# The first batch's attention values loaded once, in pairs of blocks, in a kernel of attention and two feed-forward layers

## The chip, the cores and the metric

The kernel runs on one core of one Trainium2 chip. The metric is the device time of one execution in microseconds: the median was 748.56 us over three runs (747.93 to 750.5). TensorE (PE in the rows) multiplies matrices, VectorE (DVE), ScalarE (ACT) and GpSimd (POOL) do elementwise work, and SyncE (SP) issues most of the DMAs. Each engine takes its instructions in a fixed order, and waits where one of them needs something that another engine or a DMA has not finished.

## The reference

Attention over 4 batches, 8 heads, 576 positions, head size 64, with a causal window of 64 keys; then a gated layer 512 to 2048 to 512, and a second one 512 to 1024 to 512 with a softmax gate and a layer norm. The weights are float64.

```python
rel = pos[:, None] - pos[None, :]
mask = (rel >= 0) & (rel < window)                 # window = 64
scores = np.where(mask, q @ k^T / sqrt(D), -1e9)
attn = softmax(scores);  x = (attn @ v), heads side by side     # 2304 x 512
h = x @ w_in                                       # 512 -> 2048
g = np.where(h >= 1, h, np.where(h <= -1, 0, (h + 1) ** 2 / 4))
x = g @ w_out                                      # 2048 -> 512
h = x @ w_in2;  solu = h * softmax(h)              # 512 -> 1024
out = (layernorm(solu) * g_ln) @ w_out2            # 1024 -> 512
```

## The kernel before

**Tokens.** The 2304 tokens are cut into 12 tiles `t` of 192, three to a batch, and each tile into three blocks `i` of 64 queries. The 8 heads are taken as 4 pairs, so attention has 48 steps `g` (four pairs for each tile); "pair 7" below is the step g=7, the last pair of tile 1. Two tiles make one block `j` of 384 tokens for the first layer.

**Attention of one g.** `st_qkt` transposes q and k (on TensorE while g < 12), `st_s` multiplies a block of 64 queries (of both heads) with the 128 keys that its window can reach: 64 of the block before and its own 64. So one matmul of 128 columns for each `i` (L303), except at a batch's first block, which has only 64 keys. VectorE adds `mask` and takes the row's extreme value (L311), ScalarE exponentiates (L317), VectorE takes the reciprocal of the sum (L327, L328), and GpSimd (g < 12) multiplies by it (`st_norm`, L336). `st_t` transposes the result, and `st_v` multiplies it with the value tile of this block, `vw[t, i]`: 128 keys by 512, the same 64 + 64 keys as in the scores (L370). `load_v(t)` loads a tile's three value tiles. Neighbouring blocks overlap: each of the nine blocks of a batch loads its own 128 keys, although half of them are in the tile before. The rows of 64 floats are 256 bytes each in DRAM. The tag `vw` has six buffers.

**Weights.** The first layer's weights come as 32 units of 512 KB (units are counted from 0; an even unit is a part of `w_in`, the odd one behind it the part of `w_out` for the same `f`). A unit is loaded by SP into one of five buffers `wst` (L113, L115), then turned from float64 into two float32 parts: ScalarE's `split_a` (L121), VectorE's shift and or (L125, L126), ScalarE's copy of the high part (L134), and GpSimd's subtraction for the low part (L135). The subtraction is the last reader: behind it the buffer can take the unit five further on.

**The first layer.** For each `j` and each `f` of 16, `moe_h` makes 12 matmuls into a PSUM buffer `ps_h` (two buffers), the gate runs on VectorE, ScalarE and VectorE (L399, L400, L405), and `moe_y` makes 12 more matmuls into four accumulators. "h(2)" below is `moe_h` for j=0, f=2: the first that takes all 384 tokens, and the first that needs a PSUM buffer back from the earlier gates, so it waits for the max of L405. For j=0 and f = 0, 1 the tokens are taken in two halves. Attention for later tiles and the conversion of the units are laid between these steps (`slot`, `w_conv`, `w_load`).

**Order.** The program is written in one sequence, and a list scheduler then orders each engine's instructions by its own estimate of when each can start. So an edit in one place moves instructions in others, on all engines. On SP the loads go out in one queue: a load that must wait for its buffer holds all behind it.

Of the kernel before, what the change touches and what calls it, by code (L numbers as in the profile page):

```python
# [8 lines left out]
F32 = mybir.dt.float32  # L9
# [11 lines left out]
def kernel(  # L21
# [12 lines left out]
    nc = tc.nc  # L34
    B, H, S, D = q.shape
# [6 lines left out]
    QB = TT // 64  # L42
    NTILES = NT // TT
    TPB = S // TT
# [3 lines left out]
    NF = DFF // 128  # L48
# [10 lines left out]
    mask = const.tile([128, 128], F32, name="mask")  # L59
# [8 lines left out]
    for x in range(2):  # L68
        m = mask[64 * x:64 * x + 64, :]
        nc.gpsimd.affine_select(  # L70
            out=m, in_=m, pattern=[[-1, 128]], compare_op=ALU.is_ge,
# [3 lines left out]
            out=m, in_=m, pattern=[[1, 128]], compare_op=ALU.is_gt,  # L75
# [5 lines left out]
    w_p = ctx.enter_context(tc.tile_pool(name="w", bufs=1))  # L81
    at_p = at_ctx.enter_context(tc.tile_pool(name="at", bufs=2, side="right"))
# [8 lines left out]
    def at_bank(name):  # L91
        if spare:
            spare.append(spare.pop(0))
            if spare[-1] is not None:
                return ps_acc.tile([128, 512], F32, tag=spare[-1], name=name)
        return ps_at.tile([128, 512], F32, tag="a", name=name)
# [52 lines left out]
    wih, wil, woh, wol = {}, {}, {}, {}  # L149
# [62 lines left out]
    qn, kn, qk, vw, qT, kT, xh, xl = {}, {}, {}, {}, {}, {}, {}, {}  # L212
# [5 lines left out]
    def load_qk(g):  # L218
# [29 lines left out]
                    nc.sync.dma_start(out=a[p0:p0 + 32, m0:m0 + n // 32, :], in_=s_[e])  # L248
        qk[g] = a

    def load_v(t):
        b, tl = divmod(t, TPB)
        for i in range(QB):
            w = at_p.tile([128, H, D], F32, tag="vw", bufs=6, name="vw")
            s0 = tl * TT + i * 64 - 64
            if s0 < 0:
                nc.sync.dma_start(out=w[0:64], in_=v[b, :, 0:64, :].rearrange("h p d -> p h d"))
            else:
                nc.sync.dma_start(out=w, in_=v[b, :, s0:s0 + 128, :].rearrange("h p d -> p h d"))
            vw[t, i] = w  # L260
# [2 lines left out]
    q_diag = [at_p.tile([128, QB, 2, 64], F32, bufs=1, name=f"q_diag{z}") for z in range(2)]  # L263
    for z in q_diag:
        nc.vector.memset(z, 0.0)

    def st_qkt(g):
        t, hp = divmod(g, NP)
        qt = qT[g] = q_diag[g % 2]
        kt = kT[g] = at_p.tile([128, TT + 64], F32, tag="kT", name="kT")  # L270
        if g >= NPE:
            a = qk.pop(g)
            for x in range(2):
                s_ = slice(64 * x, 64 * x + 64)
                nc.vector.transpose(qt[s_, :, x, :], a[s_, 0:6, :].rearrange("p m c -> p (m c)"))
            c0 = 0 if t % TPB else 64
            nc.vector.transpose(kt[:, c0:], a[:, 6:14 - c0 // 32, :].rearrange("p m c -> p (m c)"))
            return
        ps = at_bank("ps_t")
        c = 0  # L280
        for src in (qn, kn):
            for r in range(2):
                a = src[t, r]
                n = a.shape[0]
                nc.tensor.transpose(ps[:, c:c + n], a[:, hp * 128:hp * 128 + 128], ident[0:n, 0:n])
                c += n
        psq = ps[:, 0:TT].rearrange("c (i q) -> c i q", i=QB)
        nc.vector.tensor_copy(qt[0:64, :, 0, :], psq[0:64])
        nc.scalar.copy(qt[64:128, :, 1, :], psq[64:128])
        nc.scalar.copy(kt[:, TT + 64 - (c - TT):], ps[:, TT:c])  # L290

    def first(t, i):
        return t % TPB == 0 and i == 0

    def st_s(g):
        t, hp = divmod(g, NP)
        ps = at_bank("ps_s")
        tmp = p = at_p.tile([128, QB, 128], F32, tag="p", bufs=3, name="p")
        mx = at_p.tile([128, QB], F32, tag="mx", name="mx")
        sm = at_p.tile([128, QB], F32, tag="sm", name="sm")  # L300
        for i in range(QB):
            c0 = 64 if first(t, i) else 0
            nc.tensor.matmul(  # L303
                ps[:, i * 128 + c0:i * 128 + 128],
                qT[g][:, i, :, :].rearrange("p x q -> p (x q)"),
                kT[g][:, i * 64 + c0:i * 64 + 128],
                start=True, stop=True,
            )
        for i in range(QB):
            c0 = 64 if first(t, i) else 0  # L310
            nc.vector.tensor_tensor_reduce(  # L311
                out=tmp[:, i, c0:], in0=ps[:, i * 128 + c0:i * 128 + 128], in1=mask[:, c0:],
                scale=-0.125, scalar=3.0e38, op0=ALU.add, op1=ALU.min, accum_out=mx[:, i:i + 1],
            )
        for i in range(QB):
            c0 = 64 if first(t, i) else 0
            nc.scalar.activation(  # L317
                p[:, i, c0:], tmp[:, i, c0:], ACTF.Exp, bias=mx[:, i:i + 1], scale=-1.0,
                accum_out=sm[:, i:i + 1],
            )  # L320
        pr[g], sums[g] = p, sm
# [127 lines left out]
    spare.extend([None, None, "acc0", "acc1", "acc2", "acc3"])  # L449
    load_qk(0)  # L450
    load_v(0)
    w_load(2)
    load_qk(NP)
    load_v(1)
    w_load(3)
    st_qkt(0)
    st_qkt(1)
    for n in range(G0 + 4):
        if n <= G0:
            st_s(n)  # L460
        if 1 <= n <= G0 + 1:
            st_norm(n - 1)
        if 0 <= n - 2 <= G0:
            st_t(n - 2)
        if n == NQ:
            after(load_qk, 2 * NP)
        if n == NV:
            after(load_v, 2)
        if n + 2 <= G0 + 1:
            st_qkt(n + 2)  # L470
        if 0 <= n - 3 < G0:
            st_v(n - 3)
        if n >= NC:
            w_conv()
            w_load(1)
# [3 lines left out]
    def slots():  # L479
        for g in range(G0 + 1, NG + 1):  # L480
            if g < NG:
                st_s(g)
            yield
            st_v(g - 1)
            if g < NG:
                st_norm(g)
            yield
            if g + 1 < NG:
                st_qkt(g + 1)
            t = (g + 1) // NP  # L490
            if g + 1 >= NPE and g + 5 < NG:
                load_qk(g + 5)
            if g + 1 == NPE - 1:
                for z in range(1, 5):
                    after(load_qk, g + z + 1)
            if (g + 1) % NP == 1 and 2 < t + 1 < NTILES:
                load_v(t + 1)
            yield
            if g < NG:
                st_t(g)  # L500
            yield
# [31 lines left out]
    for n in range(len(seq) + 2):  # L533
        if n < len(seq):
            j, f, c = seq[n]
# [9 lines left out]
            if j == 1 and f == 4:  # L545
                gl_row = wk_p.tile([128, NB], F32, tag="xo", name="gl_row")[0:DF2 // 128, 0:128]
                nc.sync.dma_start(
                    out=gl_row.rearrange("k (b i) -> k b i", b=4),
                    in_=g_ln.rearrange("(b k i) -> k b i", b=4, i=32),
                )  # L550
            if j == 1 and f == 7:
                ps = at_bank("ps_g")
# [133 lines left out]
    for i in range(NI + LAG):  # L686
# [6 lines left out]
        if i < NI:  # L693
            st_ln(i)
            st_move(i)
            j, t = divmod(i, TPN)
# [37 lines left out]
```

## Time and profile before

| | |
|---|---|
| median of three runs | 748.56 us |
| profiled execution | 749.73 us |
| its span | 747.9 us (1.83 us lie around it) |
| TensorE busy in the span | 718.5 us, 96% |
| VectorE, ScalarE, GpSimd busy | 459.7, 355.1 and 142.9 us |
| mean granted clock of TensorE | 0.984 of full speed |
| moved by DMA | 92.06 MB, 117848 of 152598 packets under 512 bytes |

The span is the profiled part of one execution; the durations of single instructions are from that execution. TensorE is full over most of it, so an average over the span says little about a change at its start; the rows further down are therefore cut by stretches, by engine and by queue. `PEclk` is the clock that TensorE was granted, as a share of full speed, and the DMA share is the mean busy share of the 16 DMA engines.

### The profile page before, as it was taken

What the parts mean: (1) busy time and instruction counts of PE and PEld (TensorE: products, weight loads), DVE (VectorE), ACT (ScalarE), POOL (GpSimd) and SP (SyncE); (2) the same over time, 40 slices, a digit from 0 to 9 for tenths busy, and PEclk for the clock granted to TensorE, in tenths of its full rate; (3) what the DMA queues carried; (4) which work ended last, traced back from release to release, by engine and by line L of the source; (5) the groups of instructions that cost most, each with busy time, mean ns of one, the idle gap of its engine ahead of it and who ended that gap; (6) DMA issues with size and microseconds to landing.
All of it is one profiled execution on the core that took longest, in us unless ns stands there. A gap on an engine that the chain in (4) does not pass through costs nothing. (4 is left out here: it accounts for less than half of the span.)

```text
span 747.9 us, 12383 instructions
## 1 busy us (share of the span) xinstructions
PE 718.5 (96%) x4321; PEld 657.4 (88%) x4321; DVE 459.7 (61%) x1208; ACT 355.1 (47%) x888; POOL 142.9 (19%) x167
## 2 busy tenths in 40 slices
PE   6899789999999999999999999999998999999988
PEld 5689778999999999999999999999886887788867
DVE  3559999576666666675567654534466546476550
ACT  5777765445445444545455443422342424444441
POOL 2459766101112111211112111100100000000000
PEclk9989999999999999999999999999998999999999
DMA  9996796524335534436342103860233333433311
GB/s 190 197 250 189 209 222 157 106 66 115 80 91 147 120 82 104 111 92 125 81 105 96 40 29 100 263 243 1 85 99 139 128 127 112 143 140 129 110 44 57
DMA packets 152598, 92.06 MB, mean 123 GB/s; under 512 B 117848, under 2 KB 137048, under 8 KB 152536
## 3 DMA queue, kind: packets, MB, share of 16 engines
q1 hardware_dynamic: 143320, 69.76, 35.9%
q0 software_dynamic: 9216, 21.51, 8.5%
q8 instruction: 34, 0.56, 0.3%
q14 instruction: 28, 0.23, 0.1%
HBM read 65.54 MB, written 25.69 MB: 122 GB/s over the span
## 5 line engine op out<-in xcount | busy, mean ns | idle before, releaser
L390 PE MATMUL ps_h<-xh,wih 128*128 128x384 f32 (+1 forms) x392 | 136.6, 349 | 2.7 <-DVE u L405 2.3
L390 PE MATMUL ps_h<-xh,wil 128*128 128x384 f32 (+1 forms) x392 | 134.0, 342 | 0.0
L390 PE MATMUL ps_h<-xl,wih 128*128 128x384 f32 (+1 forms) x392 | 132.7, 339 | 1.2 <-DVE xl L378 1.1
L421 PE MATMUL acc<-gh,woh 128*128 128x384 f32 (+1 forms) x392 | 131.0, 342 | 0.0
L421 PE MATMUL acc<-gl,woh 128*128 128x384 f32 (+1 forms) x392 | 130.9, 335 | 0.0
L421 PE MATMUL acc<-gh,wol 128*128 128x384 f32 (+1 forms) x392 | 130.5, 334 | 0.0
L400 ACT ACTIVATE u<-u,half 128x384 f32<-128x384 f32 (+1 forms) x98 | 59.6, 610 | 147.0 <-DVE u L399 146.7
L399 DVE TENSOR_SCALAR u<-ps_h 128x384 f32<-128x384 f32 (+1 forms) x98 | 53.5, 547 | 85.7 <-PE ps_h L390 85.6
L390 PEld LDWEIGHTS ps_h<-xh,wih 128*128 128x128 f32 x392 | 74.7, 191 | 5.1 <-DVE u L405 2.9
L390 PEld LDWEIGHTS ps_h<-xl,wih 128*128 128x128 f32 x392 | 74.9, 191 | 1.9 <-DVE xl L378 1.7
L390 PEld LDWEIGHTS ps_h<-xh,wil 128*128 128x128 f32 x392 | 75.0, 191 | 0.8
L421 PEld LDWEIGHTS acc<-gl,woh 128*128 128x128 f32 x392 | 74.2, 189 | 0.1
L421 PEld LDWEIGHTS acc<-gh,wol 128*128 128x128 f32 x392 | 74.0, 189 | 0.0
L421 PEld LDWEIGHTS acc<-gh,woh 128*128 128x128 f32 x392 | 73.5, 190 | 0.4
L406 ACT CAST gh<-u 128x384 fp32r<-128x384 f32 (+1 forms) x98 | 49.6, 506 | 50.3 <-DVE u L405 47.9
L405 DVE TENSOR_TENSOR u<-ps_h,u 128x384 f32<-128x384 f32 (+1 forms) x98 | 52.6, 536 | 33.9 <-ACT u L400 33.7
L674 PE MATMUL ps_o<-woh,wih 128*128 128x512 f32 (+1 forms) x152 | 59.8, 393 | 5.8 <-ACT wih L662 3.1
L135 POOL TENSOR_TENSOR w2st<-wst,w2st 128x512 fp32r<-128x512 f32 x16 | 20.9, 1309 | 227.6 <-ACT w2st L134 210.3
L317 ACT ACTIVATE p<-p,mx 128x128 f32<-128x128 f32 (+1 forms) x144 | 55.2, 385 | 8.5 <-DVE mx L311 8.3
L674 PE MATMUL ps_o<-wol,wih 128*128 128x512 f32 (+1 forms) x152 | 58.8, 387 | 0.0
L674 PE MATMUL ps_o<-woh,wil 128*128 128x512 f32 (+1 forms) x152 | 58.7, 386 | 0.0
L410 DVE TENSOR_TENSOR gl<-u,gh 128x384 fp32r<-128x384 f32 x80 | 44.2, 552 | 22.5 <-ACT gh L406 22.4
(93 smaller groups left out, 1277.8 us busy)
## 6 DMA issues: line engine op xcount, KB each, us to landing
vw<-in_v_dram SPq DMA_DIRECT2D x32, 256.0 KB
wst<-in_moe_w_in_dram SPq DMA_DIRECT2D x16, 512.0 KB
wst<-in_moe_w_out_dram SPq DMA_DIRECT2D x16, 512.0 KB
w2d<-w2st POOLq DMA_DIRECT2D x16, 512.0 KB, 3.4
lnd<-e SPq DMA_DIRECT2D x15, 512.0 KB
lT<-lnd SPq DMA_DIRECT2D x60, 128.0 KB
x2d<-xo POOLq DMA_DIRECT2D x24, 192.0 KB, 2.2
x2r<-x2d SPq DMA_DIRECT2D x6, 768.0 KB
```

The costliest lines, as they stand in the source:

```text
L135: nc.gpsimd.tensor_tensor(lo, val, as_f32(hi), op=ALU.subtract)
L317: nc.scalar.activation(p[:, i, c0:], tmp[:, i, c0:], ACTF.Exp, bias=mx[:, i:i + 1], scale=-1.0, accum_out=sm[:, i:i + 1],)
L390: nc.tensor.matmul(ps, a, bb[:, kc, c], start=(n == 0), stop=(n == 3 * KC - 1))
L399: nc.vector.tensor_scalar(u, ps, -1.0, 1.0, op0=ALU.max, op1=ALU.min)
L400: nc.scalar.activation(u, u, ACTF.Square, bias=half, scale=0.5)
L405: g = nc.vector.tensor_tensor(u, ps, u, op=ALU.max)
L406: return nc.scalar.copy(hi, u).ins, g.ins
L410: eng.tensor_tensor(lo, u, as_f32(hi), op=ALU.subtract)
L421: nc.tensor.matmul(acc[j, e][:, c], a, bb, start=(f == 0 and n == 0 and c.start == 0), stop=(f == NF - 1 and n == 2),)
L674: nc.tensor.matmul(ps, a[kk // 4][:, kk % 4, :], b[kk][:, c:c + w], start=(n == 0), stop=(n == 3 * NK2 - 1),)
```

## The change

Values: for batch 0 alone, `load_v` reads the 576 rows once, as pairs of blocks that do not overlap: rows 0 to 127, 128 to 255, and so on, five loads (two for t=0, one for t=1, two for t=2) in place of nine. Four of them are 256 KB and one 128 KB, 1152 KB in all; the nine were 2176 KB. An odd block `n = 3t + i` needs the 64 keys before it and its own: that is one such pair as it stands. An even block beyond 0 needs the second half of one pair and the first half of the next. For it, GpSimd copies the two halves, 64x512 each, into a further tile (L272, L273): its own keys land in the lower half and the earlier keys in the upper. So the order of the two halves is swapped for these blocks (n = 2, 4, 6, 8), and the scores follow: two matmuls of 64 columns (L330) in place of one of 128, and a mask `mask_s` with its halves swapped. Sixteen more matmuls over the steps g = 0 to 11, eight copies on GpSimd, two small ones on VectorE for the mask, four DMAs fewer.

```diff
--- before.py
+++ after.py
@@ -248,8 +248,30 @@
                     nc.sync.dma_start(out=a[p0:p0 + 32, m0:m0 + n // 32, :], in_=s_[e])
         qk[g] = a
 
+
+
+    vpair = {}
+
+    def swapped(t, i):
+        return t < TPB and t * QB + i > 0 and (t * QB + i) % 2 == 0
+
     def load_v(t):
         b, tl = divmod(t, TPB)
+        if b == 0:
+            for m in ((0, 1), (2,), (3, 4))[t]:
+                n = min(128, S - 128 * m)
+                w = vpair[m] = at_p.tile([128, H, D], F32, tag="vw", bufs=6, name="vw")
+                nc.sync.dma_start(
+                    out=w[0:n], in_=v[b, :, 128 * m:128 * m + n, :].rearrange("h p d -> p h d")
+                )
+            for i in range(QB):
+                m = (t * QB + i) // 2
+                vw[t, i] = vpair[m]
+                if swapped(t, i):
+                    w = vw[t, i] = at_p.tile([128, H, D], F32, tag="vw", bufs=6, name="vw")
+                    nc.gpsimd.tensor_copy(w[0:64], vpair[m][0:64])
+                    nc.gpsimd.tensor_copy(w[64:128], vpair[m - 1][64:128])
+            return
         for i in range(QB):
             w = at_p.tile([128, H, D], F32, tag="vw", bufs=6, name="vw")
             s0 = tl * TT + i * 64 - 64
@@ -263,6 +285,9 @@
     q_diag = [at_p.tile([128, QB, 2, 64], F32, bufs=1, name=f"q_diag{z}") for z in range(2)]
     for z in q_diag:
         nc.vector.memset(z, 0.0)
+    mask_s = w_p.tile([128, 512], F32, tag=f"woh{NF - 1}", name="mask_s")[:, 0:128]
+    for x in range(2):
+        nc.vector.tensor_copy(mask_s[:, 64 * x:64 * x + 64], mask[:, 64 - 64 * x:128 - 64 * x])
 
     def st_qkt(g):
         t, hp = divmod(g, NP)
@@ -300,6 +325,15 @@
         sm = at_p.tile([128, QB], F32, tag="sm", name="sm")
         for i in range(QB):
             c0 = 64 if first(t, i) else 0
+            if swapped(t, i):
+                for x in range(2):
+                    nc.tensor.matmul(
+                        ps[:, i * 128 + 64 * x:i * 128 + 64 * x + 64],
+                        qT[g][:, i, :, :].rearrange("p x q -> p (x q)"),
+                        kT[g][:, i * 64 + 64 - 64 * x:i * 64 + 128 - 64 * x],
+                        start=True, stop=True,
+                    )
+                continue
             nc.tensor.matmul(
                 ps[:, i * 128 + c0:i * 128 + 128],
                 qT[g][:, i, :, :].rearrange("p x q -> p (x q)"),
@@ -309,7 +343,8 @@
         for i in range(QB):
             c0 = 64 if first(t, i) else 0
             nc.vector.tensor_tensor_reduce(
-                out=tmp[:, i, c0:], in0=ps[:, i * 128 + c0:i * 128 + 128], in1=mask[:, c0:],
+                out=tmp[:, i, c0:], in0=ps[:, i * 128 + c0:i * 128 + 128],
+                in1=(mask_s if swapped(t, i) else mask)[:, c0:],
                 scale=-0.125, scalar=3.0e38, op0=ALU.add, op1=ALU.min, accum_out=mx[:, i:i + 1],
             )
         for i in range(QB):
```

The scheduler then orders all engines anew. From the first rows of block j=1 on, the rows of both programs are in the same order on each engine. Ahead of that they differ in many places; three of them follow. The numbers in tile names only count the tiles.

SP, behind the loads of q and k for tile 1, before: the three value loads of tile 1 (`vw_162` to `vw_166`) stand ahead of units 2, 3 and 4 (`wst_170`, `174`, `178`).

```order
L236 DMA qkn_156<-in_k_dram 128x8x64
L236 DMA qkn_157<-in_k_dram 128x8x64
L259 DMA vw_162<-in_v_dram 128x8x64
L259 DMA vw_164<-in_v_dram 128x8x64
L259 DMA vw_166<-in_v_dram 128x8x64
L113 DMA wst_170<-in_moe_w_in_dram 128x4x256
L115 DMA wst_174<-in_moe_w_out_dram 128x1024
L113 DMA wst_178<-in_moe_w_in_dram 128x4x256
L236 DMA qkn_446<-in_q_dram 96x8x64
```

The same place now; units 2, 3 and 4 are `wst_173`, `177`, `181`.

```order
L236 DMA qkn_160<-in_k_dram 128x8x64
L236 DMA qkn_161<-in_k_dram 128x8x64
L113 DMA wst_173<-in_moe_w_in_dram 128x4x256
L115 DMA wst_177<-in_moe_w_out_dram 128x1024
L113 DMA wst_181<-in_moe_w_in_dram 128x4x256
L236 DMA qkn_456<-in_q_dram 96x8x64
L264 DMA vw_166<-in_v_dram 128x8x64
```

Tile 1's values are one load, and it stands behind the three units.

SP, from unit 5 on, before (units 5 to 12 are `wst_372`, `421`, `470`, `504`, `528`, `537`, `612`, `616`). The loads of `vw_482` to `486` are tile 2's values, those of `vw_679` to `683` tile 3's, whose buffers the value matmuls of pair 7 release.

```order
L115 DMA wst_372<-in_moe_w_out_dram 128x1024
L113 DMA wst_421<-in_moe_w_in_dram 128x4x256
L259 DMA vw_482<-in_v_dram 128x8x64
L259 DMA vw_484<-in_v_dram 128x8x64
L259 DMA vw_486<-in_v_dram 128x8x64
L115 DMA wst_470<-in_moe_w_out_dram 128x1024
L113 DMA wst_504<-in_moe_w_in_dram 128x4x256
L115 DMA wst_528<-in_moe_w_out_dram 128x1024
L257 DMA vw_679<-in_v_dram 64x8x64
L113 DMA wst_537<-in_moe_w_in_dram 128x4x256
L259 DMA vw_681<-in_v_dram 128x8x64
L115 DMA wst_612<-in_moe_w_out_dram 128x1024
```

The same place now; units 5 to 13 are `wst_380`, `430`, `480`, `518`, `542`, `551`, `627`, `631`, `715`, and tile 3's first value tile is `vw_696`.

```order
L115 DMA wst_380<-in_moe_w_out_dram 128x1024
L113 DMA wst_430<-in_moe_w_in_dram 128x4x256
L115 DMA wst_480<-in_moe_w_out_dram 128x1024
L264 DMA vw_492<-in_v_dram 128x8x64
L113 DMA wst_518<-in_moe_w_in_dram 128x4x256
L264 DMA vw_494<-in_v_dram 64x8x64
L115 DMA wst_542<-in_moe_w_out_dram 128x1024
L113 DMA wst_551<-in_moe_w_in_dram 128x4x256
L115 DMA wst_627<-in_moe_w_out_dram 128x1024
L113 DMA wst_631<-in_moe_w_in_dram 128x4x256
L115 DMA wst_715<-in_moe_w_out_dram 128x1024
L279 DMA vw_696<-in_v_dram 64x8x64
```

Before, the load for tile 3 stood behind unit 9; now it stands behind unit 13.

VectorE, around the reciprocal of pair 7 (`rs_659`) and the two max instructions of the second halves (`u_717`, `u_800`), the first of which frees the PSUM buffer for h(2); before. Units 5 and 6 (`wst_372`, `421`) have their shifts ahead of these rows, and unit 7 is `wst_470`.

```order
L288 COPY q_diag1_125<-ps_t_671 64x3x64
L327 TENSOR_SCALAR sm_640<-sm_640 128x3
L378 TENSOR_TENSOR xl_316<-ps_x_650,xh_315 128x192
L328 RECIPROCAL rs_659<-sm_640 128x3
L399 TENSOR_SCALAR u_717<-ps_h_704 128x192
L399 TENSOR_SCALAR u_800<-ps_h_787 128x192
L405 TENSOR_TENSOR u_717<-ps_h_704,u_717 128x192
L405 TENSOR_TENSOR u_800<-ps_h_787,u_800 128x192
L125 TENSOR_SCALAR wst_470<-wst_470 128x512
```

The same instructions now: the reciprocal is `rs_594`, the max instructions are those of `u_734` and `u_819`, unit 8 is `wst_518`, unit 9 `wst_542`, and units 12 and 13 are `wst_631` and `wst_715`.

```order
L126 SCALAR_TENSOR_TENSOR wst_518<-wst_518 128x512
L362 TENSOR_SCALAR sm_574<-sm_574 128x3
L125 TENSOR_SCALAR wst_542<-wst_542 128x512
L363 RECIPROCAL rs_594<-sm_574 128x3
...
L125 TENSOR_SCALAR wst_715<-wst_715 128x512
L434 TENSOR_SCALAR u_734<-ps_h_721 128x192
L126 SCALAR_TENSOR_TENSOR wst_631<-wst_631 128x512
L434 TENSOR_SCALAR u_819<-ps_h_806 128x192
L126 SCALAR_TENSOR_TENSOR wst_715<-wst_715 128x512
L440 TENSOR_TENSOR u_734<-ps_h_721,u_734 128x192
L440 TENSOR_TENSOR u_819<-ps_h_806,u_819 128x192
```

Unit 9's shift now stands ahead of the reciprocal of pair 7, and unit 13's shift and or ahead of the max for h(2).

## Rows read from the trace of the kernel before

**Rows 1.** stretches of 0 to 500 us: length, engines' busy time, clock, DMA share
```profile
core 0: us, PE busy (x) PEld busy (x) DVE busy (x) ACT busy (x) POOL busy (x), PEclk, DMA share, GB/s
0.00:52.00 52.00, 42.73 (x293) 36.32 (x294) 25.19 (x116) 34.14 (x116) 20.77 (x33) 0.93 0.94 205
52.00:130.00 78.00, 70.13 (x462) 65.79 (x460) 75.19 (x166) 57.13 (x139) 58.12 (x44) 0.96 0.77 202
15.00:21.00 6.00, 6.00 (x43) 4.60 (x43) 4.26 (x15) 4.99 (x20) 3.64 (x6) 1.00 1.30 206
21.00:27.00 6.00, 5.24 (x25) 4.77 (x25) 1.60 (x9) 2.60 (x11) 1.35 (x2) 1.00 1.07 299
200.00:500.00 300.00, 300.00 (x1996) 289.16 (x1996) 184.48 (x549) 140.74 (x378) 42.31 (x55) 1.00 0.42 113
```

**Rows 2.** what TensorE waited for, 0 to 130 us: total, times, longest
```profile
PE ps_p L349 <- DVE p L332: 2.8, 2, 1.8
PE ps_h L390 <- DVE u L405: 2.3, 1, 2.3
```

**Rows 3.** TensorE's timeline: start, length, engine, line, operation
```profile
51.26 0.55 PE L351 MATMUL ps_p<-ident,p 128*128 128x128 f32 x3 [0.39 <-POOL p L336]
51.64 0.83 PE L303 MATMUL ps_s<-kT,q_diag 128*128 128x128 f32 x6
52.23 0.42 PE L390 MATMUL ps_h<-xh,wih 128*128 128x384 f32 x1
134.10 0.33 PE L390 MATMUL ps_h<-xh,wih 128*128 128x384 f32 x1
```

**Rows 4.** timeline of SP's issues: start, length, line, destination and source
```profile
15.40 3.86 SPq L259 DMA_DIRECT2D vw<-in_v_dram  x3
19.30 1.12 SPq L113 DMA_DIRECT2D wst<-in_moe_w_in_dram  x1
30.60 2.44 SPq L248 DMA_DIRECT2D qk<-in_q_dram  x4
42.05 0.45 SPq L115 DMA_DIRECT2D wst<-in_moe_w_out_dram  x1
48.67 0.62 SPq L257 DMA_DIRECT2D vw<-in_v_dram  x1
```

**Rows 5.** what SP's queue waited for, 0 to 130 us
```profile
SPq L257 <- PE ps_x L370: 6.3, 1, 6.3
```

**Rows 6.** VectorE by line and shape, 57 to 120 us: busy, mean ns | idle
```profile
L126 DVE SCALAR_TENSOR_TENSOR wst<-wst 128x512 uint32<-128x512 uint32 x21 | 23.0, 1096 | 0.5 <-ACT wst L121 0.3
L125 DVE TENSOR_SCALAR wst<-wst 128x512 uint32<-128x512 uint32 x22 | 16.9, 773 | 0.5 <-DMA wst<-in_moe_w_out_dram 0.5
```

**Rows 7.** VectorE by line and shape, 130 to 250 us
```profile
L126 DVE SCALAR_TENSOR_TENSOR wst<-wst 128x512 uint32<-128x512 uint32 x5 | 3.5, 694 | 0.0
```

**Rows 8.** GpSimd by line and shape, 0 to 130 us
```profile
L135 POOL TENSOR_TENSOR wil<-wst,wih 128x512 fp32r<-128x512 f32 x16 | 24.3, 1522 | 4.2 <-ACT wih L134 4.1
L336 POOL TENSOR_TENSOR p<-p,rs 128x384 f32<-128x384 f32 x8 | 7.6, 955 | 14.5 <-PE ps_x L370 6.8 <-DVE rs L328 4.4 <-DMA qk<-in_q_dram 1.7
L336 POOL TENSOR_TENSOR p<-p,rs 128x256 f32<-128x256 f32 x4 | 2.4, 612 | 0.0
```

**Rows 9.** GpSimd's timeline; the last two are first and last of 25 units
```profile
29.19 0.83 POOL L336 TENSOR_TENSOR p<-p,rs 128x384 f32<-128x384 f32 x1 [6.84 <-PE ps_x L370]
55.76 1.67 POOL L135 TENSOR_TENSOR wol<-wst,woh 128x512 fp32r<-128x512 f32 x1 [1.40 <-ACT woh L134]
123.60 1.32 POOL L135 TENSOR_TENSOR wol<-wst,woh 128x512 fp32r<-128x512 f32 x1
```

**Rows 10.** TensorE's score matmuls by shape, 0 to 130 us
```profile
L303 PE MATMUL ps_s<-kT,q_diag 128*128 128x128 f32 x80 | 17.3, 366 | 0.8 <-ACT kT L290 0.8
L303 PE MATMUL ps_s<-kT,q_diag 128*128 128x64 f32 x16 | 4.3, 364 | 1.3 <-ACT kT L290 1.3
```

**Rows 11.** ScalarE by line and shape, 57 to 120 us
```profile
L121 ACT ACTIVATE wst<-wst 128x512 f32<-128x512 f32 x21 | 14.2, 677 | 0.0
```

## The prediction

> **What bounds the kernel now.** I read the stretches first, then what TensorE waited for, then the queues. From 200 to 500 us TensorE is busy 300.00 of 300.00 us: nothing done outside it matters there [rows 1]. In the first 52 us it is busy 42.73, in 52 to 130 us 70.13 of 78, at a granted clock of 0.93 and 0.96 of full speed (between the two levels, 1.2 and 2.4 GHz) [rows 1]. So what can be won lies before 130 us: 9.3 us idle up to 52, 7.9 us up to 130, and a clock loss of about 0.07 x 52 = 3.6 and 0.04 x 78 = 3.1 us. TensorE's waits there are for many small things, the two largest 2.8 and 2.3 us [rows 2]; no single producer stands out. Two resources stand behind them. Up to about 52 us the DMA engines are full (share 0.94 at 205 GB/s [rows 1]). From 57 to 120 us it is the conversion of the weights: between the subtractions at 55.76 and 123.60 us GpSimd does 25 units, one per 2.83 us [rows 9], and each unit's two DVE instructions take 1.10 + 0.77 us there [rows 6], where the first of them later takes 0.69 [rows 7].
>
> The yardstick is the first matmul of the second token block, h of j=1, f=0, at 134.10 us [rows 3]. Behind it both programs have the same rows in the same order on every engine, and TensorE has no idle left to absorb or give anything; so the shift at that point is the shift at the end.
>
> **The change, part by part.**
>
> *Fewer bytes.* Of 2.18 MB of batch 0's values 1.05 MB are no longer read, all in 256-byte pieces. 15 to 21 us is such a stage: 206 GB/s [rows 1], so about 5.1 us of DMA time. Ahead of unit 2 (units counted from 0) 0.13 MB and the three loads of t=1 go, 0.92 MB or 4.5 us; the latter held SP for 3.86 us, up to 19.30 [rows 4]. Units 2 to 4 are therefore issued near 15 us instead of 19.30.
>
> *More weights before the attention's last early heads.* The order on SP puts units 10 to 13 ahead of the first value load of t=3, which before stood right behind unit 9 and held the queue 6.3 us, to 48.67 [rows 4, 5]. So the ring is refilled as it empties. But it also changes VectorE's order: the reciprocal of head pair 7 stands behind unit 9's shift, and the max that frees the PSUM buffer for h(2) stands behind unit 13's. Before, that max had only units 5 and 6 ahead of it, and h(2) began at 52.23 us [rows 3].
>
> *When h(2) starts now.* Added up from the shapes of the loads in front, 9.2 MB have to land up to unit 9; at the 205 GB/s of [rows 1] that is 45.0 us. ScalarE's split (0.68 [rows 11]) and the shift (0.4 to 0.8) follow: the norm of pair 7 at about 46.3, then unit 8's subtraction (1.5 [rows 8]), whose end lets unit 13 be issued, 48.7. Up to the end of unit 13 it is 11.3 MB, 55.2 us at the same rate; three units still to land from 48.7 on give 54.0 at 299 GB/s [rows 1] and 56.4 at 205. I take 54.5, plus split, DVE's or and the two gate instructions, 2.0 us: h(2) at 56.5, with ends of 52.7 (as in rival A) and 60.
>
> *From h(2) to the yardstick.* Before 134.10 - 52.23 = 81.87 us; less the 7.87 us idle and 3.1 us of clock, 70.9 us of work. Moved behind h(2): the transposes of pair 8 (0.55) and the scores of pair 9 (three matmuls, 0.83, so 0.28 each [rows 3]). With the two more of pair 9 and two more in each of pairs 10 and 11 that is nine matmuls, 2.5 us; together 73.9. Of the 11.0 us of idle and clock loss I leave 3. Seven units (7 to 13) whose shifts before came behind this point are now ahead of it, each 1.87 us of DVE's time [rows 6]: 13.1 us taken off an engine that was the bound; what is late next is TensorE itself. So 76.9, and the yardstick at 133.4: 0.7 us earlier than 134.10.
>
> *More matmuls.* Sixteen more, of 64 columns in pairs in place of one of 128. Ten come before h(2), in a stage that waits for data, at nothing; were that cover gone, 10 x 0.28 = 2.8 us at full clock, twice that at half. Bounds for one: from 0 (two halves cost a whole) to 0.5 us. The rows decide near 0.28: 16 records of 64 columns took 4.3 us, 0.27 each, 80 of 128 columns 17.3, 0.22 each [rows 10]: no discount for half the columns. The Trainium skill (TensorE: Matmul & The Clock Gate, Back-to-back issue gap) says otherwise for a stream: about 60 cycles between matmuls up to 64 columns against 134 at 128. By that the six extra ones behind h(2) would cost nothing and the sum would be 1.7 us lower; the trace does not agree, so the sum keeps them.
>
> *GpSimd's eight copies* of 64x512. No copy stands in the trace. Two-input operations on it take 0.61 us at 256 elements, 0.96 at 384, 1.5 at 512 [rows 8]: bounds 0.6 and 1.5, I take 0.8, 6.4 us in all. GpSimd is busy 20.77 of 52 us [rows 1] and stood 6.84 us idle ahead of pair 4's norm at 29.19 [rows 9], where two of them now stand: hidden. If they are not, two cost that chain 1.6 us, and the chain then waits for the DMA anyway. The two small mask copies on DVE at the start and four fewer SP issues: nothing, DVE is busy 25.19 of 52 us.
>
> **Sum.** The profiled execution took 749.73 us for a span of 747.9; 0.7 less is 749.0. It lies 1.17 us above the median of the three runs shown (748.56), so the forecast is 747.9.
>
> **The rivals.**
>
> A, *the stage runs at the weights' rate*. If the removed waits on SP let the DMAs run at 235 GB/s (between 205 and 299 [rows 1]), unit 13 lands near 50 us, h(2) starts at 52.7, and with 1.5 us of stalls left the yardstick is at 52.7 + 75.4 = 128.1: 6.0 us earlier, 742.6. For it: 15 to 21 us at 206 GB/s and 21 to 27 at 299 show what the 256-byte pieces cost. Against it: the ring of five buffers, which lets unit 13 go only behind unit 8's subtraction.
>
> B, *VectorE holds h(2)*: slower. VectorE executes in order, and behind unit 13's or stand the max of both second halves, on which h(2) waits, and the scores' reduces of pair 9. GpSimd now runs its subtractions and copies in just this stretch, and DVE's instructions lengthen beside it (0.69 to 1.10 us [rows 6, 7]). If each of eight copies and six subtractions adds 0.4 us and the landing is at 56.4, h(2) starts at 60 or later; with 4 us of stalls left the yardstick is at 137.9, 3.8 later: 752.4. It decides from an h(2) later than 57.2 us, the break-even. The Trainium skill (SBUF — State Buffer, SBUF: two separate sides) gives the mechanism: DVE and GpSimd share a port pair under an exclusive lock, which the loser waits for over a whole instruction. By that rule eight copies of 0.8 us could hold DVE 6.4 us; the trace agrees as far as the lengthened rows show it.
>
> C, *the last weights are late*: 32 loads of q and k for pairs 13 to 16 now wait for pair 11's transposes, in h(6) near 80 us, ahead of unit 28; four such took 2.44 us of SP [rows 4], so 20 us, unit 28 at 100. Its h(14) comes near 122, with conversion some 10 us behind the landing: a stall only if the DMAs fall behind too, then some 4 us, 752.
>
> **How the numbers follow.** Forecast 0.38, A 0.33, B 0.22, C 0.07. Its own range is 744.5 to 750.5. The range for 8 in 10 reaches from A's 742.6 to B's 752.4: 742 to 752.5. About 0.3% (2.2 us) is what a measurement can tell from no change: below 746.3 is faster, above 750.8 slower. The forecast gives 0.06 faster, 0.29 same, 0.03 slower; A 0.29 and 0.04 same; B 0.20 slower and 0.02 same; C 0.06 and 0.01. Together 0.35, 0.36, 0.29.
>
> **What would show it.** In the profile after: unit 2's issue near 15 us; unit 13's near 48 and h(2) at 55 to 58, its wait on DVE's max; fewer of the units' DVE instructions in 57 to 120 us than the 21 and 22 of [rows 6], and TensorE's idle from 52 to 130 us down from 7.9 to about 2; the last subtraction well before 123.6; yardstick at 132 to 135. Wrong if h(2) starts before 54 or after 59, if idle stays at 7 us in spite of the earlier weights, or if h(14) or h(15) waits for a weight.

## The result, and the profile after

The changed kernel takes 759.51 us (757.42 to 760.03, four runs), the kernel before 748.43 in the same comparison: a ratio of 1.0137, 95% interval 1.011 to 1.0165. The change made it 11 us slower, outside the range of the forecast (742 to 752.5). The profiled execution took 759.01 us for a span of 757.2, 9.3 more than the span before; the trace accounts for these 9.3 us of the 11 between the medians.

The stretches again, to be laid beside [rows 1]; the third runs from h(2) to the yardstick (the first matmul of j=1), and the next three cut it at h(9) and h(13).

```profile
core 0: us, PE busy (x) PEld busy (x) DVE busy (x) ACT busy (x) POOL busy (x), PEclk, DMA share, GB/s
0.00:52.00 52.00, 41.28 (x296) 36.35 (x297) 32.09 (x120) 36.76 (x115) 28.76 (x42) 0.96 0.91 216
52.00:130.00 78.00, 67.60 (x444) 63.49 (x444) 65.97 (x148) 51.44 (x128) 52.59 (x43) 0.92 0.64 177
58.49:143.16 84.67, 78.23 (x513) 74.13 (x513) 66.02 (x163) 52.34 (x135) 48.85 (x41) 0.94 0.57 152
58.49:101.12 42.63, 38.78 (x252) 36.90 (x252) 39.89 (x77) 30.44 (x72) 34.90 (x27) 0.92 0.59 173
101.12:122.33 21.21, 21.21 (x148) 20.46 (x148) 12.11 (x41) 11.22 (x30) 6.69 (x8) 1.00 0.80 212
122.33:143.16 20.83, 18.24 (x116) 16.77 (x115) 14.02 (x46) 10.67 (x34) 7.26 (x7) 0.92 0.30 48
200.00:500.00 300.00, 300.00 (x2006) 288.71 (x2006) 185.09 (x555) 141.72 (x380) 42.20 (x55) 1.00 0.41 109
```

And the kernel before between the same four matmuls, same columns:

```profile
52.23:92.04 39.81, 35.83 (x242) 34.12 (x241) 38.80 (x85) 31.77 (x77) 32.86 (x25) 0.96 0.73 206
92.04:118.47 26.43, 22.55 (x139) 20.76 (x139) 25.50 (x55) 18.03 (x43) 18.54 (x16) 0.94 0.94 237
118.47:134.10 15.63, 15.63 (x109) 14.63 (x109) 12.90 (x32) 9.20 (x28) 7.74 (x6) 1.00 0.46 95
```

Up to h(9) the new stage is 2.8 us longer (42.63 against 39.81); from h(9) to h(13) it is 5.2 shorter (21.21 against 26.43, TensorE full at full clock); from h(13) on 5.2 longer (20.83 against 15.63). With h(2) 6.3 us later that gives 9.1, which is the whole shift of the yardstick and, within 0.3 us, of the span. From 200 to 500 us TensorE is full as before [rows 1].

What makes the stretches longer can be read from the same rows. Up to h(9) TensorE's idle time is no longer than before (3.9 us against 4.0). Six of the extra matmuls stand there, 1.3 us in all by what one is measured at below, and the lower granted clock (0.92 against 0.96) takes 3.4 us in place of 1.6. From h(13) on 2.6 us are idle and the clock of 0.92 takes 1.7; before, neither.

What TensorE waited for, 0 to 150 us (total, times, longest), three of its rows beside [rows 2]. A wait for the mask at the start is left out in both places: 2.8 us here, 2.7 before, which makes it the second longest there.

```profile
PE ps_h L425 <- DVE u L440: 7.1, 4, 3.2
PE ps_p L384 <- DVE p L367: 1.9, 1, 1.9
PE ps_p L386 <- POOL p L371: 1.8, 1, 1.8
```

Its timeline at h(2), at the largest wait behind it, and at the yardstick, beside [rows 3]:

```profile
58.49 0.69 PE L425 MATMUL ps_h<-xh,wih 128*128 128x384 f32 x1 [3.23 <-DVE u L440]
128.61 0.27 PE L384 MATMUL ps_p<-ident,p 128*64 128x128 f32 x1 [1.90 <-DVE p L367]
143.16 0.33 PE L425 MATMUL ps_h<-xh,wih 128*128 128x384 f32 x1
```

h(2) starts at 58.49 in place of 52.23 and waits 3.23 us for VectorE's max; the yardstick is at 143.16 in place of 134.10.

SP's issues, beside [rows 4]: unit 2, unit 13, the first value load of tile 3, the first of 32 loads of q and k, units 28, 29 and 30.

```profile
13.60 1.25 SPq L113 DMA_DIRECT2D wst<-in_moe_w_in_dram  x1
49.86 0.34 SPq L115 DMA_DIRECT2D wst<-in_moe_w_out_dram  x1
51.78 0.61 SPq L279 DMA_DIRECT2D vw<-in_v_dram  x1
86.88 1.30 SPq L248 DMA_DIRECT2D qk<-in_q_dram  x3
102.34 0.40 SPq L113 DMA_DIRECT2D wst<-in_moe_w_in_dram  x1
110.41 0.83 SPq L115 DMA_DIRECT2D wst<-in_moe_w_out_dram  x1
111.33 0.38 SPq L113 DMA_DIRECT2D wst<-in_moe_w_in_dram  x1
```

Unit 2 goes out 5.7 us earlier than before; the forecast was near 15 us, 4.3 earlier. Units 28 to 30 go out at 102 to 111 us, no earlier than before, although unit 27 was issued at 85.29.

VectorE ahead of h(2):

```profile
54.82 0.42 DVE L125 TENSOR_SCALAR wst<-wst 128x512 uint32<-128x512 uint32 x1
55.15 0.35 DVE L434 TENSOR_SCALAR u<-ps_h 128x192 f32<-128x192 f32 x1
55.42 1.05 DVE L126 SCALAR_TENSOR_TENSOR wst<-wst 128x512 uint32<-128x512 uint32 x1
56.40 0.34 DVE L434 TENSOR_SCALAR u<-ps_h 128x192 f32<-128x192 f32 x1
56.66 1.51 DVE L126 SCALAR_TENSOR_TENSOR wst<-wst 128x512 uint32<-128x512 uint32 x1
58.10 0.34 DVE L440 TENSOR_TENSOR u<-ps_h,u 128x192 f32<-128x192 f32 x1
```

Read from the end: the max at 58.10 frees the buffer; ahead of it stand unit 13's or (L126, 1.51 us), the second half's gate (L434), unit 12's or (1.05), and so on up. The gate instructions themselves were ready: TensorE had finished the halves at 55 us and stood idle.

VectorE at unit 30's landing:

```profile
121.10 0.43 DVE L125 TENSOR_SCALAR wst<-wst 128x512 uint32<-128x512 uint32 x1 [3.18 <-DMA wst<-in_moe_w_in_dram]
123.02 1.00 DVE L125 TENSOR_SCALAR wst<-wst 128x512 uint32<-128x512 uint32 x1
127.12 1.34 DVE L367 TENSOR_TENSOR p<-p,rs 128x64 f32<-128x64 f32 x1
```

It waits 3.18 us for a weight's DMA (unit 30's), and then two units' shifts and ors, a pair's reduces and transposes and a gate's two instructions stand, almost without idle time between them, ahead of a norm that ends at 128.5, on which TensorE waits 1.90 us (128.61 above).

### The profile page after: what moved, and what is told of

It is laid out like the page before. It is cut to its first block, busy times and chain, and to the rows that moved or that the text cites. A ratio compares the mean times of both kernels' runs of the same rounds, so it can differ in the third digit from the quotient of the medians.

```text
span 757.2 us, 12455 instructions
## 1 busy us (share of the span) xinstructions
PE 722.4 (95%) x4353; PEld 661.8 (87%) x4353; DVE 460.7 (61%) x1210; ACT 355.3 (47%) x888; POOL 146.2 (19%) x175
## 5 line engine op out<-in xcount | busy, mean ns | idle before, releaser
L434 DVE TENSOR_SCALAR u<-ps_h 128x384 f32<-128x384 f32 (+1 forms) x98 | 53.5, 546 | 88.0 <-PE ps_h L425 88.0
```

What stands on the lines that cost most here:

```text
L434: nc.vector.tensor_scalar(u, ps, -1.0, 1.0, op0=ALU.max, op1=ALU.min)
```

## The experiments

Five theories. **O**: order; the scheduler put units 9 to 13 ahead of the attention's and gates' instructions on VectorE, so h(2) is late. **G**: GpSimd's eight copies hold the attention chain. **M**: the extra matmuls cost it. **L**: the last units are late behind the q and k loads. **V**: VectorE's pace sets the stage from h(2) on. All kernels are scheduled anew after an edit, so none changes its part alone; the starts of h(2), h(9), h(13), h(14) and of the yardstick (j=1), found by laying each kernel's order of matmuls on its trace, show where each gained or lost. In swap_by_dma and no_copies 18 more matmuls stand ahead of h(2), so their h(2) is not the same point of the work. The ratios are to runs of the kernel before in the same comparison, whose medians were 747.9 to 748.7.

```
kernel                  median   ratio to before (95%)     h(2)  h(9)  h(13) h(14)  j=1
before                  748.4                              52.2  92.0 118.5 123.5 134.1
after                   759.5   1.0137 (1.0110..1.0165)    58.5 101.1 122.3 131.4 143.2
pin_units               750.9   1.0037 (1.0023..1.0052)    53.9  95.6 119.7 124.7 135.3
swap_by_dma             753.3   1.0075 (1.0053..1.0097)    60.9  97.2 121.9 127.0 138.1
no_copies               750.8   1.0042 (1.0025..1.0059)    54.0  92.6 118.6 125.2 136.3
copies_only             754.7   1.0087 (1.0063..1.0112)    57.9  99.6 120.9 126.9 138.1
before_held             756.0   1.0090 (1.0070..1.0110)    51.2  96.9 124.4 130.7 141.8
after_weights_first     754.7   1.0069 (1.0049..1.0089)    56.8  99.7 122.9 127.9 139.9
before_weights_first    751.3   1.0045 (1.0028..1.0062)    51.5  91.3 118.9 125.7 136.7
pin_weights_first       750.2   1.0027 (1.0009..1.0045)    53.6  95.3 116.9 124.0 136.1
pin_earlier             748.7   1.0012 (0.9998..1.0026)    51.4  93.0 117.1 122.2 133.2
pin_earlier_weights     751.1   1.0048 (1.0028..1.0069)    55.1  96.8 120.7 126.4 136.9
before_one_shift        744.3   0.9949 (0.9933..0.9966)    52.4  87.4 112.8 118.0 129.9
after_one_shift         746.4   0.9978 (0.9963..0.9992)    54.4  93.0 114.2 120.1 130.4
```

**pin_units**: only the order on VectorE. `pins[1]` is the max of the step before; `issue_after` queues what is written under it behind that instruction on its engine.

```diff
             slot(n0)
-            w_conv()
+            if n - 1 in (2, 3):
+                with tc.issue_after(pins[1]):
+                    w_conv()
+            else:
+                w_conv()
             pins = moe_g2(*part)
...                                   # the second w_conv() of a step likewise, for n in (2, 3)
```

> The changed kernel with one thing held: on VectorE the shifts of units 10 and later stand behind the max instructions of the second halves, on which h(2) waits. Loads, copies and extra matmuls stay. Theory O (order: h(2) is late because units 9 to 13 stand ahead of its max on VectorE): h(2) starts at 53 to 55 us in place of 58.5, and the time falls to 749 to 753. Theory G (GpSimd's eight copies hold the attention chain and VectorE): nothing but noise, 757 to 760, with h(2) still behind 57.

750.9 us: 8.6 of the 11 us are gone by the medians, three quarters of the loss by the ratios, with every copy, load and extra matmul in place, and h(2) is back at 53.88, its wait halved:

```profile
53.88 0.44 PE L425 MATMUL ps_h<-xh,wih 128*128 128x384 f32 x1 [1.58 <-DVE u L440]
```

O holds for h(2), and G falls: the copies are all there. But the same edit also let the scheduler put the q and k loads behind unit 23 instead of unit 27, so the 8.6 us are not h(2)'s alone.

**swap_by_dma**: the value tiles of even blocks by two DMAs, no copies and no bytes saved.

```diff
+                if swapped(t, i):
+                    nc.sync.dma_start(out=w[0:64], in_=v[b, :, s0 + 64:s0 + 128, :]...)
+                    nc.sync.dma_start(out=w[64:128], in_=v[b, :, s0:s0 + 64, :]...)
...                                   # the loads of pairs of blocks are taken out
```

> No GpSimd copies and no bytes saved: the even blocks' value tiles are loaded from DRAM as two DMAs of 64 rows in swapped order, the scores are those of the changed kernel (16 more matmuls of 64 columns). Theory G: without copies the loss is gone, 748 to 750. Theory O: here unit 11 stands ahead of the max for h(2), and nothing is saved in bytes, so h(2) is at 56 or later and the time 753 to 760. Theory M (the extra matmuls cost it): 753 or more, with h(2) at 54 and the time lost spread over the scores.

753.3 us. Without any copy the loss is still 5 us: against G again, and in O's range, though at its lower end and with other matmuls ahead of h(2). The time alone would suit M too (753 or more), but h(2) is not at 54 as M said.

**no_copies**:

```diff
...                                   # every pair is loaded with 128 rows
                 if swapped(t, i):
-                    w = vw[t, i] = at_p.tile([128, H, D], F32, tag="vw", bufs=6, name="vw")
-                    nc.gpsimd.tensor_copy(w[0:64], vpair[m][0:64])
-                    nc.gpsimd.tensor_copy(w[64:128], vpair[m - 1][64:128])
+                    pass
```

> The changed kernel without the eight GpSimd copies: an even block takes the pair's tile as it is, so half of its values are the wrong rows; the last pair is loaded whole (128 KB more). The bytes saved and the extra matmuls stay. Theory G: 746 to 749. Theory O: only unit 10 stands ahead of the max for h(2), so h(2) near 54 to 56 and the time 749 to 754. Theory M: 752 or more.

750.8 us, as O said (749 to 754), and M's 752 or more is missed: the extra matmuls are in. With fewer bytes and no copies it is still slower than before.

**copies_only**:

```diff
-            if swapped(t, i):
-                for x in range(2):
-                    nc.tensor.matmul(...)       # two of 64 columns
-                continue
...
-                in1=(mask_s if swapped(t, i) else mask)[:, c0:],
+                in1=mask[:, c0:],
```

> The changed kernel without the extra matmuls: the scores are computed as before, by one matmul of 128 columns and the old mask, on value tiles in swapped order, so the even blocks' results are wrong. Bytes saved and eight copies stay. Theory M: the loss is gone, 748 to 750. Theory O: unit 13 stands ahead of the max for h(2) as in the changed kernel, so h(2) at 57 to 59 and the time 756 to 760. Theory G: the same, 756 to 760.

754.7 us: below O's range, though h(2) waits as O said, at 57.93 for 5.22 us:

```profile
57.93 0.69 PE L413 MATMUL ps_h<-xh,wih 128*128 128x384 f32 x1 [5.22 <-DVE u L428]
```

M's 748 to 750 is further off. The other 4.8 us against the changed kernel are only in part the price of 16 matmuls: h(9) comes 1.5 us earlier, but 3.0 us more are won in the step from h(13) to h(14), where none of the extra matmuls stands: 6.1 us for 9.1. What the matmuls cost is read directly, from pair 4's scores: in the changed kernel one of 128 columns, two of 64 and one of 128 (two records for each matmul).

```profile
30.51 0.49 PE L337 MATMUL ps_s<-kT,q_diag 128*128 128x128 f32 x2
30.84 0.56 PE L330 MATMUL ps_s<-kT,q_diag 128*128 128x64 f32 x4
31.23 0.44 PE L337 MATMUL ps_s<-kT,q_diag 128*128 128x128 f32 x2
```

The same pair in the kernel before, three of 128 columns:

```profile
29.71 0.94 PE L303 MATMUL ps_s<-kT,q_diag 128*128 128x128 f32 x6
```

At the granted clock of 1.00 in both places, the records of 64 columns start 0.11 us apart (30.89, 31.00, 31.12), and those of 128 columns do too (30.04, 30.15, 30.26 before). At 49 us, where the clock was 0.50, it is 0.21 us for 64 columns. So here a matmul of half the columns takes as long as a whole one, 0.22 us at the full clock, and that is what a swapped block costs more: 1.3 us for the six behind h(2).

**before_held**: the kernel before, with one edge.

```diff
...                                   # `shifted` collects every unit's or
-            pins = moe_g2(*part)
+            if n == 2:
+                with tc.issue_after(shifted[-1]):      # unit 9's or
+                    pins = moe_g2(*part)
+            else:
+                pins = moe_g2(*part)
```

> The kernel before, with one thing imposed: the max that frees the PSUM buffer for h(2) is queued on VectorE behind unit 9's shift and or. Nothing else is edited: loads, values and matmuls are those of before. Theory O (order on VectorE is what delays h(2) and so the end): unit 9's shift came at 55.6 us, so h(2) at 56 to 57 in place of 52.2 and the time 751 to 754. Theory G (copies, or anything of the change's own work): 747 to 749, since none of it is in.

756.0 us: the loss of O without the change, and more than O said. The scheduler let the other half's max go first, so h(2) took that buffer and h(3) the held one. VectorE and TensorE there:

```profile
56.30 1.51 DVE L127 SCALAR_TENSOR_TENSOR wst<-wst 128x512 uint32<-128x512 uint32 x1
57.73 0.34 DVE L406 TENSOR_TENSOR u<-ps_h,u 128x192 f32<-128x192 f32 x1
```

```profile
58.13 0.69 PE L391 MATMUL ps_h<-xh,wih 128*128 128x384 f32 x1 [3.40 <-DVE u L406]
```

One edge of order, with nothing added to the work, costs 7.3 us here, a wait of 3.40 us and what grows from it. This is the strongest run for O, although the wait is at h(3) and not at h(2).

**after_weights_first**, **before_weights_first** and **pin_weights_first**: q and k of pairs 15 to 18 behind unit 31 on SP; in the changed kernel, in the one before, and in pin_units.

```diff
-            if g + 1 >= NPE and g + 5 < NG:
+            if g == NPE + 1:
+                with tc.issue_after(wdma[31]):
+                    for z in range(2, 6):
+                        load_qk(g + z)
+            elif g > NPE + 1 and g + 5 < NG:
                 load_qk(g + 5)
             if g + 1 == NPE - 1:
-                for z in range(1, 5):
+                for z in range(1, 4):
                     after(load_qk, g + z + 1)
```

> The changed kernel with the loads of q and k for pairs 15 to 18 queued behind unit 31, so that units 28 to 31 follow after 16 instead of 32 such loads. Theory L (the last units are late behind the q and k loads, and that is the 9 us step from h(13) to h(14)): h(2) stays at 58.5, that step shrinks to 5 to 6 us, the time is 754 to 756. Theory O alone: the end is set by h(2) and by VectorE's pace, 758 to 760.

754.7 us, in L's range. SP issues units 28 and 31 at 92.79 and 95.36 (102.34 and 111.81 before the edit), and GpSimd's last subtraction starts at 111.22 in place of 127.1:

```profile
92.79 0.39 SPq L113 DMA_DIRECT2D wst<-in_moe_w_in_dram  x1
95.36 0.34 SPq L115 DMA_DIRECT2D wst<-in_moe_w_out_dram  x1
```

```profile
111.22 1.61 POOL L135 TENSOR_TENSOR wol<-wst,woh 128x512 fp32r<-128x512 f32 x1 [3.75 <-ACT woh L134]
```

The step from h(13) to h(14) is 5.0 us in place of 9.1; the next two are 6.0 and 5.9 in place of 6.6 and 5.2. So 3.8 us are won behind h(13), of 16 us by which the last unit is earlier; 2.0 are lost between h(9) and h(13), which takes 23.2 us in place of 21.2. Another 1.7 us stand already at h(2), though every engine has the same instructions in the same order up to there: so much differs from one execution to the next.

> The kernel before with the same edit: q and k of pairs 15 to 18 behind unit 31. Theory L says that the kernel before has little of this stall, since its units wait for the ring and its q and k loads are spread: 746 to 749. If the 9.3 us step from h(12) to h(13) in it has the same cause, 743 to 745.

751.3 us, a miss: slower than before. The last weights are not what made the kernel before slow there; its slow steps are now h(9) to h(11), 8.4 and 8.0 us.

> The changed kernel with both edits: units 10 and later behind the max for h(2) on VectorE, and q and k of pairs 15 to 18 behind unit 31. Theories O and L together: h(2) at 54, no step above 7 us behind h(9), 745 to 748, no slower than the kernel before. O without L: 750 to 752, as with the first edit alone.

750.2 us, in the range of O without L: once units 10 and later are held, this edit adds nothing that the intervals can tell.

**pin_earlier** and **pin_earlier_weights**: the conversions of three steps are taken together behind the second halves' max, so that only units 5 and 6 stand ahead of it; the second also queues q and k of pairs 15 to 17 behind unit 28.

```diff
+            if n == 3:
+                with tc.issue_after(pins[1]):
+                    for _ in range(5):
+                        w_conv()            # not called in steps 1, 2 and at the head of 3
```

> The changed kernel with VectorE's order around h(2) made like that of before: only units 5 and 6 ahead of the max instructions of the second halves, units 7 to 11 behind them; the value load of tile 3 comes behind unit 11 again earlier than unit 12. Theory O in full (all of the loss is order): h(2) at 52 to 53, and with the bytes saved 744 to 748. If the work moved and added (nine score matmuls, eight copies) is not repaid by the bytes: 749 to 751, as with the pin at unit 10.

748.7 us, ratio 1.0012 (0.9998 to 1.0026): no slower than before that can be told, and not faster. h(2) starts at 51.41:

```profile
51.41 0.69 PE L425 MATMUL ps_h<-xh,wih 128*128 128x384 f32 x1 [0.97 <-DVE u L440]
```

So with this order no loss is left that can be told, though every copy and every extra matmul is in. The 744 to 748 of "O in full" is missed: the megabyte that is not read brings no gain that can be told, net of what the copies and matmuls cost. What each of the two is worth by itself is not shown.

> The same with q and k of pairs 15 to 17 queued behind unit 28. Theory L: the step from h(12) to h(14) loses another 1 to 3 us against the kernel without this edit, 743 to 748. If VectorE's pace sets the stage whatever the loads do, the same as that kernel within 1 us.

751.1 us, a miss for L: with the pin in place the weights need no help, and the new schedule (h(2) at 55.1) costs 2.4 us.

**before_one_shift** and **after_one_shift**: one VectorE instruction for a unit in place of two.

```diff
-        nc.vector.tensor_scalar(low, low, 29, None, op0=ALU.logical_shift_right)
-        nc.vector.scalar_tensor_tensor(
-            high, high, 3, low, op0=ALU.logical_shift_left, op1=ALU.bitwise_or
-        )
+        nc.vector.tensor_scalar(high, high, 3, None, op0=ALU.logical_shift_left)
```

> The kernel before with one VectorE instruction for a unit in place of two: the shift alone, without the or of the low word (the three lowest bits of each weight's mantissa are left out). It takes about 1.1 us for each unit from VectorE. Theory V (VectorE sets the pace from h(2) to h(13)): 740 to 744. If it does not, and waits for loads or ScalarE stand right behind it: 746 to 749.

744.3 us, 0.3 above V's range; the range of the other reading began at 746.

> The changed kernel with the same edit; units 12 and 13 still stand ahead of the max for h(2) on VectorE. Theory V: 743 to 748, the step from h(2) to h(9) falls from 42.6 to 37 us or less, and the difference to the kernel before with this edit shrinks from 11 to 3 to 6 us (h(2) stays late by landing). If the difference stays at 9 to 12: VectorE's pace has no part in the loss, only h(2) and the last units.

746.4 us: the difference between the two kernels falls from 11 to 2 us, less than V's 3 to 6. h(2) to h(9) takes 38.6 us in place of 42.6, not the 37 that V said. VectorE from 52 to 100 us in before, in before_one_shift and in after_one_shift (third number):

```profile
52.00:100.00 48.00, 43.17 (x292) 40.83 (x290) 46.96 (x98) 37.29 (x87) 38.78 (x29) 0.96 0.74 205
```

```profile
52.00:100.00 48.00, 46.42 (x326) 43.85 (x326) 31.11 (x95) 38.29 (x96) 35.97 (x31) 0.98 0.70 196
```

```profile
52.00:100.00 48.00, 45.65 (x310) 44.35 (x311) 31.33 (x83) 34.95 (x86) 32.99 (x29) 0.91 0.62 182
```

Before, VectorE is busy 46.96 of 48 us; with one shift 31 of 48, and TensorE 3.3 us more in the same stretch. This bears V out for the kernel before: work taken off VectorE becomes work done on TensorE. With room on VectorE the same change costs a fifth. But the edit also takes the ors from ahead of the max for h(2), which came at 54.4 and did not stay late as had been expected; so the second run does not separate V from O. The edit leaves three low bits of every first-layer weight out; its two versions are the only ones that come out below the kernel before (0.9949, and 0.9978 at 0.9963 to 0.9992).

## Why the prediction was wrong

**The step that failed** is "Of the 11.0 us of idle and clock loss I leave 3." From h(2) to the yardstick TensorE was busy 78.23 of 84.67 us at a clock of 0.94: 6.4 us idle and 5.1 us of clock, 11.5 in all. Nothing of the 11.0 went away. The work beside it, 73.9 us in the forecast, measured 84.67 - 11.5 = 73.2. Against the forecast yardstick of 133.4 that makes 9.8 us: 2.0 from h(2) and 8.5 from idle and clock, less 0.7 of work.

The argument was that seven units' shifts moved ahead of h(2) free an engine that was the bound. Over the whole stage they did: VectorE was busy 66.0 us of it in place of 77.2, and from 57 to 120 us it did fewer of the units' instructions than [rows 6] have, 17 and 16 for 21 and 22, the sign that the prediction had named:

```profile
L126 DVE SCALAR_TENSOR_TENSOR wst<-wst 128x512 uint32<-128x512 uint32 x17 | 21.5, 1272 | 2.0 <-ACT wst L121 1.8
L125 DVE TENSOR_SCALAR wst<-wst 128x512 uint32<-128x512 uint32 x16 | 10.9, 680 | 0.6 <-DMA wst<-in_moe_w_in_dram 0.6
```

But it was not thinned out where it was needed. Between h(2) and h(9) it did units 14 to 27, 14 units where before it did 15 (7 to 21): SP issued these units one behind the other up to 85.29 us as the buffers came free, and the scheduler places what is ready. VectorE was busy 39.89 of 42.63 us there (38.80 of 39.81 before), and a unit's two instructions took 2.05 us in the mean (1.87 before), with GpSimd busy 82% of the time in both. The relief came only when the ring ran dry, with no unit issued from 85.29 to 102.34: from h(9) to h(13) TensorE was full and 5.2 us were won. They were lost again behind h(13). TensorE's idle time from 52 to 130 us, which was to fall to 2 us, came to 10.4.

**h(2).** Forecast 56.5, measured 58.49; unit 13 was issued at 49.86 (forecast 48.7). The mechanism was right and the size 2 us off. One or of 0.69 us had been added up; two stood ahead of the max, and took 1.05 and 1.51 us. GpSimd at that time:

```profile
55.05 0.87 POOL L371 TENSOR_TENSOR p<-p,rs 128x384 f32<-128x384 f32 x1 [0.38 <-ACT kT L315]
55.89 1.74 POOL L135 TENSOR_TENSOR wol<-wst,woh 128x512 fp32r<-128x512 f32 x1
```

Each or started beside one of these and ended 0.55 us after it. Part of the 2 us is the execution: in after_weights_first the same order gave h(2) at 56.77.

**Rivals B and C happened, both.** B, VectorE holding h(2), had 0.22, with h(2) at 60 and 752.4; C, the last units behind 32 q and k loads, had 0.07 and 752. pin_units and before_held show B, after_weights_first shows C, 3.8 us behind h(13) where C had said 4. They were priced as cases that exclude each other, and B took the stage behind h(2) as 77.9 us, where it measured 84.67. A did not happen: unit 2 went out early, but in the first 52 us the DMAs moved 216 GB/s and not 235, and h(2) waited for VectorE.

**The copies** were cheap: 0.65 to 0.70 us each, against an estimate of 0.8; the sum had left them out as hidden.

```profile
L273 POOL COPY vw<-vw 64x512 f32<-64x512 f32 x4 | 2.8, 699 | 8.8 <-DMA vw<-in_v_dram 6.6 <-PE ps_x L405 2.1
L272 POOL COPY vw<-vw 64x512 f32<-64x512 f32 x4 | 2.6, 650 | 0.3 <-PE ps_x L405 0.3
```

Not all were hidden. One stood ahead of pair 4's norm and waited 2.11 us for TensorE's last use of its buffer; the norm came at 31.42 in place of 29.19 [rows 9]. By pair 7's norm nothing of that is left against the forecast, 46.44 for 46.3:

```profile
30.72 0.61 POOL L273 COPY vw<-vw 64x512 f32<-64x512 f32 x1 [2.11 <-PE ps_x L405]
31.42 0.82 POOL L371 TENSOR_TENSOR p<-p,rs 128x384 f32<-128x384 f32 x1
46.44 1.70 POOL L371 TENSOR_TENSOR p<-p,rs 128x384 f32<-128x384 f32 x1 [1.81 <-PE acc L456]
```

**The extra matmuls** were priced nearly right, at 0.28 us each. That figure is a third of the busy time of three in [rows 3]; from start to start one takes 0.22 us at the full clock, so nine were some 0.5 us too dear, most of the 0.7 us by which the work came out lower. [rows 10] count records, two to a matmul, and mix both clock levels, but "no discount for half the columns" holds. The Trainium skill (TensorE: Matmul & The Clock Gate, Back-to-back issue gap) gives about 60 cycles up to 64 columns against 134 at 128 as the gap of matmuls by themselves. The trace does not agree, with 0.11 us between records at either width, each of which has a weight load of its own (64 loads for the 64 records of 64 columns); the prediction was right to leave that price out.

**Fewer bytes** were counted as earlier weights, and that was right: unit 2 at 13.60. That earlier weights are worth time was not borne out. no_copies and pin_earlier both save the bytes and neither is faster than before.

## What to carry to other kernels

In a program that a list scheduler orders, data that arrives earlier can become work that is placed earlier, on engines that take it in order; ask what stands behind it there, and pin the instructions that the bounding engine waits for. Work that moves ahead relieves an engine only if no other work of the same kind takes its place: count what the engine does in each stretch, not what has been done by its start. Two rivals that do not rule each other out can both happen, and then their prices add.

## What the runs showed of the hardware

GpSimd's copy of 64 partitions by 512 floats took 0.60 us undisturbed (0.65 and 0.70 mean), its two-input subtraction over 128 partitions by 512 elements 1.30.

VectorE's two-input or over 128x512 took 0.65 to 0.70 us in the changed kernel's 20 rows that no GpSimd instruction overlaps, its one-input shift 0.41 to 0.43 in 27 such rows. Beside GpSimd they reached 2.09 and 1.55 us. All 17 ors longer than 0.9 us ended 0.55 or 0.56 us after the end of a GpSimd instruction, and all 11 shifts longer than 0.65 us 0.28 or 0.29 us after one; in the kernel before the same holds for 17 and 12. The Trainium skill (SBUF — State Buffer, SBUF: two separate sides) has the loser wait for a whole instruction, and the trace agrees: the longest or started at 40.46 us, stood through the rest of a copy and the whole subtraction behind it, up to 41.99, and ended 0.56 us later.

A float32 score matmul of 64 columns took as long as one of 128: records 0.11 us apart at the full clock, 0.21 at a granted 0.50.
